# Layer 2's raw weights on GpSimd's DMA queue, their conversion's arithmetic behind the next step's gating

## The chip, the cores and the metric

One Trainium2 chip, one core of it. The metric is the device time of one launch in microseconds. The kernel before was run three times.

## The reference

Three parts follow one another on 3072 tokens of width 512, in float32; the inputs are given as 64-bit floats.

```python
for t in range(S):                       # B 4, H 8, S 768, D 64
    state = gamma * state + outer(k[t], v[t])
    y[t] = scale * q[t] @ state          # linear attention with decay per head
x = y as [3072, 512]
h = x @ w_in;  g = h * sigmoid(1.702 * h);  x = g @ w_out         # layer 1: 512 -> 2048 -> 512
h = x @ w_in2; P = a0 + a1 h + a2 h^2 + a3 h^3
Q = 1 + |b0| |h| + |b1| h^2;  out = (P / (Q + 1e-6)) @ w_out2     # layer 2: 512 -> 2048 -> 512
```

## The kernel before

Matrix products are made from a high and a low float32r part of each operand: three matmuls per product (high x low, low x high, high x high). So weights and activations must be split. A raw 64-bit weight is first turned into one float32 word by bit operations on ScalarE and VectorE.

Layer 1 runs in 96 steps: six blocks of 512 tokens, in each 16 chunks of 128 of the 2048 hidden columns. `step(i)` (L1538) works on two chunks at once: it issues the up-projection `g1(j)` of chunk j = i + 2 (12 matmuls of 128x512, L1122), its gating `act1_a(j)` (sigmoid on ScalarE, L1229; product z on VectorE, L1230), later the split of z into gh and gl by `act1_b(j)` (ScalarE L1238, VectorE L1239), and the down-projection `g2(i)` of chunk i (12 matmuls, L1143 to L1145). The up-projection's result stands in one of two PSUM banks (pool `ps_h`, tag "h", which attention's output `py` shares), so a bank is free for the next but one `g1` when z has been read out of it.

Between these stand the items of `todo[i]`: from block 1 on, attention's later chunks. `att_unit(c)` (L929) makes 64x64 matmuls (L954) for chunk c and chunk c + 1, then has SP fetch the turned q and k of c + 2 (`att_fetch`, L831) and load the raw q and k of c + 3 and the raw v of c + 2 (`load_raw`, L735). `att_turn(c)` (L812) scales and transposes q and k on VectorE (L816, L818) and has SP store them to DRAM (L823). The positions are counted in half-steps of a block (`UNIT_AT`, `TURN_IN`, L722 and L723): units at 1, 9, 17 and 25 with a turn 7 later; in the first such block, units at 9, 15, 21 and 25 and turns 5, 5, 3 and 7 later.

The conversion of layer 2's weights also runs beside layer 1: eight groups g, each of two chunks of w_in and two of w_out (units 4g to 4g + 3, 512 KB of raw words each). `conv2(g, x)` (L662) is the work of position x of a group, from x = -1 to 9; it is called at the end of step i with x = i - conv0[g] (L1573 to L1580), and conv0 is nine steps apart for the first groups and eight for the last. A raw unit is loaded by `raw2` (L622) at x = -1, 0, 3 and 5; `word2` (L634) makes the float32 word of it (ScalarE L561, then four operations on VectorE: L567, L569, L572, L583) at x = 0, 2, 5 and 7; `parts` and `whole` split it (ScalarE L619, VectorE L620), at x = 3 after four sums (L682); `put` (L649) stores the split weight to DRAM on GpSimd's queue at x = 2, 4, 6, 8 and 9, once per unit and once for the sums. Raw units, sums and other scratch share four slots (pool `ws`, tag "s"); a slot is free when the store that reads it has landed. `evac` takes two of them at the end of each block.

Each engine and each DMA queue works through its instructions in order. From step 14 to step 77 the orders of TensorE, VectorE, ScalarE and SP are the order in which the code issues them (`manual_schedule`, L1585); GpSimd's order isn't among them, but a DMA under `behind` (L613) stays after everything issued before it on its own engine. From step 78 on a planner orders all engines; there the sums and splits of layer 2's input are made (`x_piece`). Then layer 2 runs, from weights that it loads back from DRAM.

Of the kernel before, what the change touches and what calls it, by code (L numbers as in the profile page):

```python
# [18 lines left out]
P = 128  # L19
# [4 lines left out]
KD = DM // P  # L24
# [447 lines left out]
def tile_kernel(ctx: ExitStack, tc: tile.TileContext, q, k, v, w1i, w1o, w2i, w2o, pa, pb, cst, out):  # L472
    nc = tc.nc
# [47 lines left out]
    def unit(layer, u):  # L521
        return (ORD if layer == 1 else ORD2)[u]

    def stage_tag(u):

        if u < 16:
            at_slot = 31 - u
        elif u < 24:
            at_slot = 47 - u
        elif u < 28:  # L530
            at_slot = 55 - u
        elif u == 30:
            at_slot = 31
        else:
            return None
        return f"w{at_slot}"
# [49 lines left out]
    def w_high(layer, u, whole=True):  # L586
        nm, fc = unit(layer, u)
        if whole and layer == 1 and u in LATER:
            return
        m = STG[u]  # L590
        shape = [P, KD, P] if nm == "i" else [P, DM]
        if nm == "i":
            m = m.rearrange("p (c f) -> p c f", c=KD)
        pair = wp.tile([P, 2, *shape[1:]], F32R, tag=f"w{u}", name=f"w{nm}{layer}_{fc}")
        STG[u] = m
        W[layer, nm, fc] = (pair[:, 0], pair[:, 1])
        high = nc.scalar.copy(out=pair[:, 0], in_=m)
        if not whole:
            tc.keep_in_program_order(high)

    def w_low(layer, u, whole=True):
        if whole and layer == 1 and u in LATER:
            return
        hi, lo = W[layer, *unit(layer, u)]
        low = nc.vector.tensor_tensor(out=lo, in0=STG.pop(u), in1=hi.bitcast(F32), op=ALU.subtract)  # L605
        if not whole:
            tc.keep_in_program_order(low)

    NG = KF // 2
# [3 lines left out]
    def behind(dma):  # L613

        tc.keep_in_program_order(dma)
# [6 lines left out]
    def raw2(u):  # L622

        nm, f = unit(2, u)
        src = {"i": w2i, "o": w2o}[nm].bitcast(I32)
        s = ws.tile([P, DM, 2], I32, tag="s", name=f"s2_{u}")
        if nm == "i":
            src = src[:, f * 2 * P : (f + 1) * 2 * P].rearrange("(c p) f -> p c f", p=P)
            behind(nc.sync.dma_start(out=s.rearrange("p (c f) t -> p c (f t)", c=KD), in_=src))
        else:  # L630
            behind(nc.sync.dma_start(out=s.rearrange("p f t -> p (f t)"), in_=src[f * P : (f + 1) * P, :]))
        STG[u] = RW[u] = s

    def word2(u):  # L634
        w_first(u)
        w_bits(u)
        w_sign(u, False)
# [4 lines left out]
    def parts(key, src, home):  # L642

        n = src.shape[1] // (2 * P)
        t = home.bitcast(F32R).rearrange("p a b -> p (a b)").rearrange("p (x h c) -> p x h c", x=n, h=2)
        split((t[:, :, 0], t[:, :, 1]), src.rearrange("p (x c) -> p x c", c=2 * P))
        OUT2[key] = t

    def put(key):  # L649
        t = OUT2.pop(key)  # L650
        g, x = key
        if x == "o":
            nc.gpsimd.dma_start(out=WO[g], in_=t.bitcast(F32))
        else:
            nc.gpsimd.dma_start(out=WC[g][x].rearrange("x p h k f -> p x (h k f)"), in_=t.rearrange("p x h c -> p x (h c)").bitcast(F32))

    def whole(f, src, home):
        t = home.bitcast(F32R).rearrange("p a b -> p (a b)").rearrange("p (h c) -> p h c", h=2)
        split((t[:, 0], t[:, 1]), src)
        OUT2[f, "o"] = t  # L660

    def conv2(g, x):  # L662

        u = 4 * g
        if x == -1:
            raw2(u)
        elif x == 0:
            raw2(u + 1)
            word2(u)
        elif x == 1:  # L670
            parts((g, 0), STG[u], RW.pop(u))
        elif x == 2:
            put((g, 0))
            word2(u + 1)
        elif x == 3:
            raw2(u + 2)
            a, b = STG.pop(u), STG.pop(u + 1)
            a11, a12, a21, a22 = a[:, : 2 * P], a[:, 2 * P :], b[:, : 2 * P], b[:, 2 * P :]
            t = SUM[g] = ws.tile([P, 4, 2 * P], F32, tag="s", name=f"sum{g}")
            A22S[g] = a22  # L680
            for y, p, q, op in ((0, a21, a22, ALU.add), (1, t[:, 0], a11, ALU.subtract), (2, a11, a21, ALU.subtract), (3, a12, t[:, 1], ALU.subtract)):
                nc.vector.tensor_tensor(out=t[:, y], in0=p, in1=q, op=op)  # L682
            parts((g, 1), t[:, 0:2].rearrange("p x c -> p (x c)"), RW.pop(u + 1))
        elif x == 4:
            put((g, 1))
        elif x == 5:
            raw2(u + 3)
            word2(u + 2)
            t = SUM.pop(g)
            parts((g, 2), t[:, 2:4].rearrange("p x c -> p (x c)"), RW.pop(u + 2))  # L690
            parts((g, 3), A22S.pop(g), t[:, 0:2])
        elif x == 6:
            put((g, 2))
            put((g, 3))
        elif x == 7:
            word2(u + 3)
            e = ws.tile([P, DM, 2], I32, tag="s", name=f"wo{2 * g}s")
            whole(2 * g, STG.pop(u + 2), e)
        elif x == 8:
            put((2 * g, "o"))  # L700
            whole(2 * g + 1, STG.pop(u + 3), RW.pop(u + 3))
        elif x == 9:
            put((2 * g + 1, "o"))
# [409 lines left out]
    def g1(j):  # L1113
        layer, bi, fc, t0, n = steps[j]
        hp = ps_h.tile([P, n], F32, tag="h", name=f"hp{j}")
        wh, wl = W[layer, "i", fc]
        xh, xl = X[layer, bi]
        terms = [(kk, w, x) for kk in range(KD) for w, x in ((wl, xh), (wh, xl), (wh, xh))]
        if j == 0:
            terms.sort(key=lambda t: ((t[2] is xl) + (t[1] is wl or t[2] is xl), t[0]))  # L1120
        for x, (kk, w, t) in enumerate(terms):
            nc.tensor.matmul(hp, w[:, kk, :], t[kk // 2][:, kk % 2, :], start=(x == 0), stop=(x == len(terms) - 1))  # L1122
        HP[j] = hp
# [100 lines left out]
    def act1_a(j):  # L1224
        n = steps[j][4]
        hp = HP.pop(j)
        z = ch.tile([P, n], F32, tag="z", name=f"z{j}")
        CH[j] = z
        nc.scalar.activation(out=z, in_=hp, func=ACTF.Sigmoid, scale=1.702)  # L1229
        nc.vector.tensor_tensor(out=z, in0=hp, in1=z, op=ALU.mult)  # L1230
# [54 lines left out]
    for u in range(NU):  # L1285
        t = stage_tag(u)
# [10 lines left out]
    with tc.manual_schedule(engines={E.SP}):  # L1297
# [207 lines left out]
        conv0 = [KF + 2 + 9 * g - (0, 0, 0, 0, 1, 2, 3, 4)[g] for g in range(NG)]  # L1505
# [13 lines left out]
        def x_piece(i):  # L1519
            left = 2  # L1520
            while xq and left and (xq[0][0] or i > XS0 + 8):
# [10 lines left out]
                else:  # L1532
                    left -= 1
                    for f in xr[s, kk][n]:
                        if f:
                            f()

        def step(i):  # L1538
            nonlocal nxt, j
            while nxt < NS and nxt - lead[steps[nxt][0]] <= i:  # L1540
                j = nxt
                nxt += 1
                g1(j)
                act1_a(j)
            if 0 <= i - KF + 2 < WHOLE:
                w_high(1, LATER[i - KF + 2], False)
                w_low(1, LATER[i - KF + 2], False)
            if i == KF:
                tc.keep_in_program_order(nc.scalar.activation(out=ab[:, 6:7], in_=ab[:, 5:6], func=ACTF.Abs))
            late = [f() for f in todo[i][0]]  # L1550
            if j >= FIRST_STEPS + 2 and j in CH:
                act1_b(j)
            for f in late:
                if f:
                    f()
            g2(i)
            layer, bi, fc, t0, n = steps[i]
            if fc == KF - 1 and bi < 5:
                evac(bi)
            late = [f() for f in todo[i][1]]  # L1560

            if i >= XS0:
                x_piece(i)
            if i >= NS - 4:
                load_wo(2 * (i - NS + 4))
                load_wo(2 * (i - NS + 4) + 1)
            if i == XS0 + 4:
                for kk in range(2):
                    t = xp.tile([P, 2, 512], F32, tag=f"xh{kk}_0", name=f"xb{kk}")
                    XB.append(t)  # L1570
                    for c in range(2):
                        nc.sync.dma_start(out=t[:, c], in_=x2[4][2 * c + kk])
            for g in range(NG):  # L1573
                x = i - conv0[g]
                if x == 9:
                    conv2(g, x)
            for g in range(NG):
                x = i - conv0[g]
                if -1 <= x < 9:
                    conv2(g, x)  # L1580
            for f in late:
                if f:
                    f()
# [4 lines left out]
        for i in range(XS0, NS):  # L1588
            step(i)
# [32 lines left out]
```

## Time and profile before

| | |
|---|---|
| time, median of 3 | 1193.75 us (1192.49 to 1194.94) |
| the profiled execution | 1192.8 us, span 1191.0 us |
| TensorE busy | 1119.5 us, 94% of the span |
| VectorE busy | 868.8 us, 73% |
| ScalarE busy | 655.2 us, 55% |
| GpSimd busy | 31.1 us, 3% |
| DMA, SP's queue (hardware) | 169.27 MB, 49.4% of 16 engines |
| DMA, GpSimd's queue (software) | 23.07 MB, 5.3% of 16 engines |

The profile is of one execution. Its times count from the span's start. "L561" is line 561 of the code, PE is TensorE, PEld its weight loads, DVE VectorE, ACT ScalarE, POOL GpSimd, SPq the queue of SP. "a <- b" reads "a waited for b". The granted clock is given as a share of full speed: 1.00 is 2.4 GHz. Issuing a DMA isn't counted as busy time on SP.

### The profile page before, as it was taken

To read this page: it belongs to the slowest core of one execution; us is meant where nothing else is said; L and a number is where in the kernel's file an instruction comes from. 1 tells how busy PE (TensorE), PEld (TensorE's weight loads), DVE (VectorE), ACT (ScalarE), POOL (GpSimd) and SP (SyncE) were. 2 spreads that over 40 slices of the span, in tenths; PEclk is the share of its full clock that TensorE was granted. 3 is DMA by queue.
4 is the path that set the end of the run, shared out by engine and by line. 5 is a ranking of instruction groups with operands and counts; after the bars stand their busy time and mean duration, and the time that the engine had idled before them with its cause. 6 is when DMAs were issued, how large, how long until landed. Compare 5 with 4: busy or idle time off the path is not lost.

```text
span 1191.0 us, 18828 instructions
## 1 busy us (share of the span) xinstructions
PE 1119.5 (94%) x7217; PEld 911.8 (77%) x7217; DVE 868.8 (73%) x1192; ACT 655.2 (55%) x987; POOL 31.1 (3%) x52
## 2 busy tenths in 40 slices
PE   8999999698996879797999999999999999999998
PEld 6688878577775757586888888888888888888887
DVE  6999646375564445455577679999889899789895
ACT  5998322132232322222354569978778786787782
POOL 0000000000000000000000000000000000000000
PEclk9999999889998989899999999999999999999999
DMA  9944557565564554565278798583345561354100
GB/s 238 326 129 115 113 127 164 151 159 153 139 157 133 141 147 120 156 168 160 95 261 297 230 325 286 195 297 153 91 129 153 184 247 46 122 157 122 43 36 36
DMA packets 230394, 193.54 MB, mean 163 GB/s; under 512 B 153888, under 2 KB 178976, under 8 KB 230304
## 3 DMA queue, kind: packets, MB, share of 16 engines
q1 hardware_dynamic: 223904, 169.27, 49.4%
q0 software_dynamic: 6400, 23.07, 5.3%
q8 instruction: 57, 0.93, 0.3%
q14 instruction: 33, 0.27, 0.1%
HBM read 134.48 MB, written 57.67 MB: 161 GB/s over the span
## 4 chain that ended last, share of the span: by engine, by line
PE 66%; SPq 11%; DMA 9%; DVE 5%; issue 3%; ACT 2%; DVEq 0%; ACTq 0%
PE o L256 22%; PE hp L1122 13%; PE a L157 11%; SPq L735 7%; PE c L157 5%; DMA s<-in_moe_w_out_dram 4%; PE o L1143 3%; PE o L1144 3%; PE o L1145 3%; PE b L157 3%; DMA s<-in_moe_w_in_dram 2%; DMA xs<-x 2%; SPq L831 2%; SPq L823 1%; PE pY L954 1%
## 5 line engine op out<-in xcount | busy, mean ns | idle before, releaser
L1122 PE MATMUL hp<-xh,wi 128*128 128x512 f32 x768 | 266.7, 410 | 44.5 <-DVE z L1230 42.8
L1122 PEld LDWEIGHTS hp<-xh,wi 128*128 128x128 f32 x768 | 150.8, 196 | 81.8 <-DVE z L1230 45.9
L1122 PE MATMUL hp<-xl,wi 128*128 128x512 f32 x384 | 154.8, 404 | 0.0
L157 PE MATMUL a<-x,wi 128*128 128x512 f32 x576 | 145.3, 390 | 0.0
L1143 PE MATMUL o<-gh,wo 128*128 128x512 f32 x368 | 144.5, 393 | 0.0
L1144 PE MATMUL o<-gl,wo 128*128 128x512 f32 x368 | 143.6, 390 | 0.0
L1145 PE MATMUL o<-gh,wo 128*128 128x512 f32 x368 | 143.4, 390 | 0.0
L567 DVE TENSOR_SCALAR u<-u 128x512 f32<-128x512 f32 x64 | 27.0, 422 | 139.7 <-ACT u L561 139.7
L561 ACT ACTIVATE u<-s 128x512 f32<-128x512 f32 x64 | 43.1, 675 | 151.7 <-DMA s<-in_moe_w_in_dram 86.7
L157 PEld LDWEIGHTS a<-x,wi 128*128 128x128 f32 x576 | 108.0, 188 | 22.9 <-ACT b L180 0.4
L1238 ACT CAST gh<-z 128x512 fp32r<-128x512 f32 x80 | 49.6, 620 | 99.6 <-DVE z L1230 99.6
L1229 ACT ACTIVATE z<-hp 128x512 f32<-128x512 f32 x80 | 47.6, 595 | 86.3 <-PE hp L1122 80.1
L1230 DVE TENSOR_TENSOR z<-hp,z 128x512 f32<-128x512 f32 x80 | 54.9, 686 | 44.8 <-ACT z L1229 36.7
L1122 PEld LDWEIGHTS hp<-xl,wi 128*128 128x128 f32 x384 | 75.9, 198 | 15.2 <-issue 0.3
L320 DVE SCALAR_TENSOR_TENSOR z<-z,ab,w 128x1024 f32<-128x1024 f32 x48 | 61.6, 1283 | 28.4 <-ACT w L318 28.4
L1143 PEld LDWEIGHTS o<-gh,wo 128*128 128x128 f32 x368 | 69.7, 189 | 15.1 <-DVE wo L605 0.4
L1239 DVE TENSOR_TENSOR gl<-z,gh 128x512 fp32r<-128x512 f32 x80 | 54.7, 684 | 36.1 <-ACT gh L1238 35.0
L1144 PEld LDWEIGHTS o<-gl,wo 128*128 128x128 f32 x368 | 69.4, 189 | 14.6 <-DVE gl L1239 0.2
L1145 PEld LDWEIGHTS o<-gh,wo 128*128 128x128 f32 x368 | 69.2, 188 | 14.5
L157 PE MATMUL c<-x,wi 128*128 128x512 f32 x288 | 73.1, 389 | 0.0
L334 ACT ACTIVATE gh<-h 128x1024 fp32r<-128x1024 f32 x48 | 50.9, 1060 | 34.1 <-PE o L256 33.5
L338 DVE SCALAR_TENSOR_TENSOR gl<-h,gh 128x1024 fp32r<-128x1024 f32 x48 | 58.8, 1224 | 5.4 <-ACT gh L334 5.4
(246 smaller groups left out, 2203.5 us busy)
## 6 DMA issues: line engine op xcount, KB each, us to landing
wi<-wc SPq DMA_DIRECT2D x168, 256.0 KB, 2.9
s<-in_moe_w_in_dram SPq DMA_DIRECT2D x32, 512.0 KB, 5.6
s<-in_moe_w_out_dram SPq DMA_DIRECT2D x32, 512.0 KB, 5.2
x<-xc SPq DMA_DIRECT2D x28, 512.0 KB, 8.5
wc<-s POOLq DMA_DIRECT2D x24, 512.0 KB, 3.9
xc<-xo SPq DMA_DIRECT2D x36, 256.0 KB, 2.7
x<-os SPq DMA_DIRECT2D x20, 256.0 KB, 2.5
xs<-x SPq DMA_DIRECT2D x20, 256.0 KB, 4.3
```

Of the source, the lines that this page charges most:

```text
L157: nc.tensor.matmul(bank, wt[:, a, k], XT[s, x, k][:, b], start=begin and y == 0, stop=y == 5, skip_group_check=True)
L256: nc.tensor.matmul(ACC[d], a[:, x, r], w[:, b], start=g == 0 and x == 0 and y == 0, stop=g == NG - 1 and x == 1 and y == 2)
L320: dve("q", [("ab", m)], lambda: stt(out=v["z"], in0=v["z"], scalar=ab[:, 6:7], in1=v["w"], op0=ALU.mult, op1=ALU.add))
L334: nc.scalar.activation(out=GT[m][0], in_=h, func=ACTF.Copy, scale=-1.0)
L338: nc.vector.scalar_tensor_tensor(out=gl, in0=h, scalar=-1.0, in1=gh.bitcast(F32), op0=ALU.mult, op1=ALU.subtract)
L735: nc.sync.dma_start(out=t[HALF[n], NP * x : NP * x + NP, :], in_=heads[x])
L1122: nc.tensor.matmul(hp, w[:, kk, :], t[kk // 2][:, kk % 2, :], start=(x == 0), stop=(x == len(terms) - 1))
L1143: nc.tensor.matmul(o, wl[:, r], gh, start=a, stop=False)
L1144: nc.tensor.matmul(o, wh[:, r], gl, start=False, stop=False)
L1145: nc.tensor.matmul(o, wh[:, r], gh, start=False, stop=z)
L1230: nc.vector.tensor_tensor(out=z, in0=hp, in1=z, op=ALU.mult)
L1239: nc.vector.tensor_tensor(out=gl, in0=z, in1=gh.bitcast(F32), op=ALU.subtract)
```

## The change

The raw units of layer 2 are loaded from GpSimd's queue, not SP's. `conv2` is cut in two: `conv2_load` issues the load of a position where `conv2` was called, at the end of step i; the arithmetic and the stores of that position are called by `convert(i - 1)` in the next step, behind its `g1` and `act1_a` and ahead of its attention items, its `act1_b` and its `g2`.

```diff
         if nm == "i":
...
-            behind(nc.sync.dma_start(out=s.rearrange("p (c f) t -> p c (f t)", c=KD), in_=src))
+            behind(nc.gpsimd.dma_start(out=s.rearrange("p (c f) t -> p c (f t)", c=KD), in_=src))
         else:
-            behind(nc.sync.dma_start(out=s.rearrange("p f t -> p (f t)"), in_=src[f * P : (f + 1) * P, :]))
+            behind(nc.gpsimd.dma_start(out=s.rearrange("p f t -> p (f t)"), in_=src[f * P : (f + 1) * P, :]))
...
+    def conv2_load(g, x):
+
+        n = {-1: 0, 0: 1, 3: 2, 5: 3}.get(x)
+        if n is not None:
+            raw2(4 * g + n)
+
     def conv2(g, x):
         u = 4 * g
-        if x == -1:
-            raw2(u)
-        elif x == 0:
-            raw2(u + 1)
+        if x == 0:
             word2(u)
...
         elif x == 3:
-            raw2(u + 2)
...
         elif x == 5:
-            raw2(u + 3)
             word2(u + 2)
...
+        def convert(i):
+            for g in sorted(range(NG), key=lambda g: i - conv0[g] != 9):
+                if 0 <= i - conv0[g] <= 9:
+                    conv2(g, i - conv0[g])
+
         def step(i):
...
                 g1(j)
                 act1_a(j)
+            convert(i - 1)
...
             for g in range(NG):
-                x = i - conv0[g]
-                if x == 9:
-                    conv2(g, x)
-            for g in range(NG):
-                x = i - conv0[g]
-                if -1 <= x < 9:
-                    conv2(g, x)
+                conv2_load(g, i - conv0[g])
```

## Rows read from the trace of the kernel before

**Rows 1.** Times by stage: from:to, length, busy of each engine, clock, DMA share, GB/s.
```profile
160.00:630.00 470.00, 406.70 (x3426) 334.07 (x3425) 261.43 (x477) 133.96 (x251) 29.10 (x45) 0.93 0.57 153
600.00:630.00 30.00, 30.00 (x134) 24.86 (x133) 23.67 (x44) 15.67 (x28) 2.59 (x5) 1.00 0.66 245
630.00:692.00 62.00, 61.73 (x272) 50.55 (x271) 41.62 (x67) 29.61 (x51) 1.83 (x3) 1.00 0.83 284
```
**Rows 2.** Waits of TensorE, 160 to 630 us: total, times, longest.
```profile
PE hp L1122 <- DVE z L1230: 42.5, 9, 9.6
PE pY L954 <- DVE z L1230: 17.2, 6, 4.1
PE pK L954 <- DMA rawv<-in_v_dram: 3.1, 1, 3.1
```
**Rows 3.** Waits of ScalarE for layer 2's raw weights, same stretch.
```profile
ACT u L561 <- DMA s<-in_moe_w_in_dram: 86.7, 7, 15.5
...
ACT u L561 <- DMA s<-in_moe_w_out_dram: 56.5, 8, 10.4
```
**Rows 4.** The chain of waits, 205 to 240 us: start, length, what.
```profile
215.40 5.46 PE hp L1122 x12
...
223.63 2.72 PE hp L1122 x12
...
232.64 4.73 DMA s<-in_moe_w_in_dram
237.39 0.67 ACT u L561
...
238.88 0.70 DVE u L572
```
**Rows 5.** SP's queue in order of time, one attention round: start, length.
```profile
216.71 1.78 SPq L823 DMA_DIRECT2D tq<-turnq  x4
...
220.52 1.66 SPq L831 DMA_DIRECT2D qT<-tq  x2
...
223.96 2.84 SPq L735 DMA_DIRECT2D rawq<-in_q_dram  x4
...
229.57 2.96 SPq L735 DMA_DIRECT2D rawv<-in_v_dram  x4
232.64 1.09 SPq L629 DMA_DIRECT2D s<-in_moe_w_in_dram  x2
```
**Rows 6.** Attention's matmuls (L954) by stage: busy and count, TensorE first.
```profile
160.00:200.00 40.00, 4.40 (x256) 4.12 (x256) 1.00 0.60 148
160.00:630.00 470.00, 41.93 (x1904) 39.11 (x1904) 0.93 0.57 153
```
**Rows 7.** GpSimd in order of time: start, length, idle before.
```profile
196.94 0.72 POOL L655 DMA_DIRECT2D wc<-s  x1 [10.85 <-DVE s L620]
197.66 0.57 POOL L655 DMA_DIRECT2D wc<-sum  x1
```
**Rows 8.** DMA issues, KB each, median us to landing; last, of L629's loads.
```profile
wc<-s POOLq DMA_DIRECT2D x24, 512.0 KB, 3.9
...
rawk<-in_k_dram SPq DMA_DIRECT2D x64, 64.0 KB, 2.7
...
tq<-turnq SPq DMA_DIRECT2D x64, 64.0 KB, 1.8
...
DMA to landing us min/median/max: 3.8/4.9/6.3
```
**Rows 9.** Groups by line, whole span: count, busy us, mean ns.
```profile
L1239 DVE TENSOR_TENSOR gl<-z,gh 128x512 fp32r<-128x512 f32 x80 | 54.7, 684 | 36.1 <-ACT gh L1238 35.0 <-PE o L1145 0.7
...
L1238 ACT CAST gh<-z 128x512 fp32r<-128x512 f32 x80 | 49.6, 620 | 99.6 <-DVE z L1230 99.6
...
L572 DVE SCALAR_TENSOR_TENSOR u<-u,s 128x512 int32<-128x512 int32 x64 | 44.3, 693 | 3.9 <-ACT s L555 0.2
...
L567 DVE TENSOR_SCALAR u<-u 128x512 f32<-128x512 f32 x64 | 27.0, 422 | 139.7 <-ACT u L561 139.7
...
L818 DVE STREAM_TRANSPOSE turnk<-rawk 128x512 f32<-128x512 f32 x16 | 11.4, 711 | 0.6
```

## The prediction, made before the change was run

> **What bounds the kernel now.** I read the times by stage first, then the waits of the engine that is full elsewhere, then one stall in the chain of waits, then the queue that it names. TensorE is full at the end of layer 1, every microsecond of 600 to 630 and 61.73 of the 62.00 after. From 160 to 630 us it works 406.70 of 470.00 us at a mean granted clock of 0.93 [rows 1]. So 63.3 us are idle there, and part of the busy time ran at the lower of its two levels, 1.2 GHz: one group of 12 matmuls took 5.46 us right after a stall, and 2.72 us when none had gone before [rows 4]. How much that is: in 160 to 200 us, at clock 1.00, 256 small attention matmuls took 4.40 us, 0.0172 each; a large one takes 2.72/12 = 0.2267. The 3426 matmuls of the stage hold 1904 small ones [rows 6], so 1522 large: 1522 x 0.2267 + 1904 x 0.0172 = 345.0 + 32.7 = 377.7 us. Busy was 406.7, so the low clock cost 29.0 us. Stall and clock together: 92.3 us that this stage would not need.
>
> Why it stalls: 42.5 + 17.2 us of 63.3 wait for VectorE's gating product z (L1230), 15 times [rows 2]; in the same stretch ScalarE waits 15 times, 143.2 us, for a raw weight of layer 2 to land [rows 3]. The chain shows how one becomes the other: raw weight on its way at 232.64, landed 237.39, ScalarE's first conversion op then, VectorE's conversion at 238.88 [rows 4]; the next step's sigmoid and z stand behind them on their queues, and a PSUM bank is free only after z. And the weight is late because its issue on SP stands behind a whole attention round: turn stores from 216.71, fetches from 220.52, 12 raw q/k/v loads from 223.96, and only at 232.64 the weight [rows 5]: 15.9 us of queue ahead of a transfer that lands in 4.9 [rows 8].
>
> **The change, part by part.**
> 1. *32 loads leave SP.* SP no longer puts them behind attention rounds. What is left in front of them is Pool's queue, which holds only the conversion's own stores, 48 of them at 0.72 us (two-part weights) or 0.57 (one part) [rows 7]. On Pool a load of w_in is four pieces of 128 rows; with 0.57 for 128 and 0.72 for 256 I estimate 0.57 + 3 x 0.15 = 1.0 us of issue, w_out 0.57. Not shown by the trace: a load from this queue. Its landing I bound by 3.8 (the fastest raw load from SP) and 6.3 (the slowest), and take 4.9, the middle of rows of the same bytes [rows 8].
> 2. *How early they now come.* Each load's slot (four of them) comes free when a store has landed: store issue 0.7, landing 3.9 [rows 8], load 1.0, landing 4.9: 10.5 us after the data of that store are ready. A step is 24 matmuls, 5.44 us, so 1.9 steps. By the schedule the stores' data are made at x = 1, 3 and 5, and the loads that they make room for are used at x = 5, at 7 and at 0 of the next group: four steps on, three for the last where groups are eight steps apart. 3 x 5.44 = 16.3 against 10.5 plus at most one step in which the data are made, 15.9: covered everywhere, by 0.4 us at the tightest (three or four places), by 5 us elsewhere. I price it at nothing; without cover it costs its excess four times.
> 3. *Arithmetic behind the next step's gating.* Nothing added or dropped; ScalarE and VectorE get each step's conversion after z(j) and ahead of the split of z(j), instead of ahead of z(j+1). A late weight would now hold up the split, not z. The split's deadline is the down-projection of j, four groups of 12 after the up-projection of j: 10.9 us. Longest load in front of it: sigmoid and product, like gh and gl, 1.3; word2 0.67 on ScalarE and 2 x 0.42 + 2 x 0.69 = 2.2 on VectorE; two part splits, 1.1 more on VectorE; a turn of four ops of at most 0.71, 2.8; then gh 0.62 and gl 0.68 [rows 4, 9]: 9.4 us. Covered by 1.5 us; without cover some 2 us in the heaviest step of each of 8 groups, 16 us. Below nothing it can't go, since the loads already take away what z waited for; I take 0 to 3.
> 4. *Pool's stores* are issued as soon as their data are there, as now, but stand behind loads that may wait for a slot. Nobody but the next loads and the far-off layer 2 waits for them.
>
> *What is late next.* Attention's ring on SP: turn 2.8, its stores 3.8, landing 1.8, fetch 3.4, raw q and k 2/3 of 8.7 = 5.8, landing 2.7 [rows 5, 8, 9]: 20.3 us per unit, to the next turn. TensorE needs 4 x 5.44 + 119 x 0.0172 = 23.8 us per unit: covered by 3.5. Only in the first block, where the turn at position 20 holds up the loads of the unit at 21 and the unit at 25 needs its raw v, it isn't: 5 x 2.72 + 2.0 = 15.6 us against turn to landed raw v, 2.8 + 3.8 + 1.8 + 3.4 + 8.7 + 2.7 = 23.2. That leaves a stall of 7.6 us, which the wait of TensorE for raw v, 3.1 us today [rows 2], grows into; with one group at the low clock after it (5.46 - 2.72 = 2.7) some 10 us. To that I add 5 us for landings that lengthen because the same bytes move in less time (DMA share 0.57 x 470/378 = 0.71; it was 0.83 in the next stage, where nothing stalled [rows 1]); the 5 is an estimate from the spread of 3.8 to 6.3.
>
> Sum against the profiled execution: 1192.8 us (span 1191.0 and 1.8 around it) - 92.3 + 10 + 5 = 1115.5. That execution lies 0.95 under the median of three, 1193.75: forecast 1116.5, say 1117 us.
>
> *A rule that speaks against.* Row first: 15.9 us of issues stand before the weight on SP, and the transfer itself is 4.7 [rows 4, 5]. The Trainium skill, "DMA: Bandwidth & Descriptors", section "Issuing engines are not separate DMA queues", says that DMAs of all issuing engines share the same 16 engines and that issuing from several saves only the sequencer's issue time, usually small. By it the gain would be the issues alone, rival E below. The trace agrees that bytes aren't the limit here (share 0.57 [rows 1]), but issue time is not small: it is what is long. So I keep the sum.
>
> **Rivals.**
> - *A, SP's attention ring becomes the pace.* For: the DMAs now overlap, and the ring has 3.5 us of room. Against: SP loses 32 issues. If its issues and landings, 17.5 of the 20.3, get 40% longer, the ring is 27.3, 3.5 over, for 16 units 56 us, and 10 for the first block: 1192.8 - 92.3 + 66 = 1166.
> - *B, slower: Pool's queue turns into a serial ring.* Place: the four slots in 160 to 630. If each load waits for the landing of the store just issued, and the next store for that load's arithmetic, a group costs 4 x (0.7 + 3.9 + 1.0 + 4.9) + 4 x 3 of arithmetic = 54 us, against 9 x 5.44 + 2.25 x 2.0 = 53.5 of TensorE: just hidden. It decides from landings a third longer: the ring is then 66, and 8 x 12 eats the 92. At landings half as long again it is 71.6, 18 x 8 = 145 us of stalls: 1192.8 - 92.3 + 145 = 1245. Against: loads are issued two steps ahead, so the ring isn't serial. The Trainium skill, "SBUF — State Buffer", section "SBUF: two separate sides", says that descriptors of a Pool DMA can't be written while VectorE holds the shared port in its two-port mode; the stores so far took 0.72 and 0.57 beside a VectorE that is busy 261 of 470 us [rows 1, 7], so no row shows it.
> - *C, no effect: the loads are as late as now*, held behind stores that wait for arithmetic: 1194. Against: point 2.
> - *D, the split of z comes late* (point 3): 1117 + 16 and the clock after each stall, 8 x 2.7: 1155.
> - *E, only the issues are saved*: the weights then wait for bytes among attention's instead of behind its issues; 32 x 0.5 us [rows 5]: 1192.8 - 16 = 1177. Against: a DMA share of 0.57 in this stage.
>
> **How the numbers follow.** Forecast 0.72, A 0.10, E 0.03, D 0.05, C 0.03, B 0.07. The forecast's own range is 1101 (all 92 us gone) to 1135 (residue twice as large). With D and the nearer half of A it reaches 1150; left out are half of A, E, B, C and a little at the edges, under 2 in 10: 1099 to 1150. What a measurement of this kernel can tell from no change is 0.2%, 2.4 us. Faster: forecast, A, E, D: 0.90; same: C and a little, 0.03; slower: B, 0.07.
>
> **What would show it.** Right: in the stage after 160 us TensorE idles under 20 us, its clock is 0.97 or more, and the stage is 70 to 90 us shorter; ScalarE's waits for raw weights fall from 143 to under 15 us; SP's rounds end with raw v; what stall is left stands in the first attention block and names raw v or a turn. Layer 2, full before [rows 1], is unchanged. Wrong: waits of u for s remain, now from Pool's loads, with Pool idle on a store's landing (B, C); ScalarE or VectorE waiting on attention's raws in every unit (A); TensorE waiting for gl at the down-projection (D).

## The result, and the profile after

The changed kernel takes 1117.08 us (median of 4, 1116.53 to 1119.67) against 1194.35 for the kernel before, timed beside it: a ratio of 0.9357, interval 0.9336 to 0.9379. The forecast was 1117. The span of the profiled execution fell from 1191.0 to 1114.8 us, by 76.2.

Times by stage of the changed kernel (length, busy of TensorE, its weight loads, VectorE, ScalarE, GpSimd, then clock, DMA share, GB/s). The work that filled 160 to 630 us [rows 1] now fills 160 to 553:

```profile
160.00:553.00 393.00, 386.90 (x3435) 320.02 (x3434) 261.97 (x477) 134.30 (x251) 49.28 (x76) 0.99 0.68 181
...
200.00:240.00 40.00, 35.06 (x358) 28.76 (x357) 22.58 (x41) 10.51 (x22) 5.03 (x8) 0.91 0.77 190
240.00:280.00 40.00, 38.84 (x392) 31.89 (x391) 27.16 (x49) 13.18 (x25) 5.21 (x8) 1.00 0.69 190
280.00:553.00 273.00, 273.00 (x2275) 226.21 (x2274) 185.62 (x340) 98.01 (x183) 36.32 (x56) 1.00 0.69 186
```

About as many TensorE instructions as in [rows 1] (3435 and 3426, with the window's edges) take 77 us less. From 280 to 553 us TensorE isn't idle for a moment, and what is left of the stall stands in 200 to 280 us. VectorE and ScalarE do the same work as before, 262 and 134 us. Behind this stage nothing changed: 561.8 us to the end of the span, 561.0 before.

The waits of TensorE in that stage, which answer to [rows 2]:

```profile
PE pK L955 <- DMA rawv<-in_v_dram: 4.9, 3, 2.0
PE o L1144 <- DVE os L1156: 1.2, 1, 1.2
```

The 59.7 us for z are gone; raw v, 3.1 us before, is the main wait. All waits of ScalarE and VectorE for layer 2's raw weights, 143 to 600 us (143.2 us on ScalarE in [rows 3]):

```profile
DVE s L569 <- DMA s<-in_moe_w_out_dram: 5.4, 2, 2.8
ACT u L561 <- DMA s<-in_moe_w_out_dram: 2.1, 1, 2.1
DVE s L569 <- DMA s<-in_moe_w_in_dram: 0.7, 1, 0.7
```

GpSimd in order of time (start, length, idle before and what ended it): stores and loads in turn, and a load that waits 2.87 us for a store to land, as the prediction's point 2 has it:

```profile
183.36 0.71 POOL L655 DMA_DIRECT2D wc<-s  x1 [13.53 <-DVE s L620]
184.07 0.58 POOL L631 DMA_DIRECT2D s<-in_moe_w_out_dram  x1
199.84 0.72 POOL L655 DMA_DIRECT2D wc<-s  x1 [15.20 <-DVE sum L620]
200.56 0.58 POOL L655 DMA_DIRECT2D wc<-sum  x1
204.01 0.75 POOL L629 DMA_DIRECT2D s<-in_moe_w_in_dram  x1 [2.87 <-DMA wc<-s]
```

SP's queue in the first attention block: this round ends with raw v, and the next one follows at once, so SP has no room here:

```profile
214.67 1.00 SPq L832 DMA_DIRECT2D qT<-tq  x2
...
217.35 2.77 SPq L736 DMA_DIRECT2D rawq<-in_q_dram  x4
...
222.89 2.57 SPq L736 DMA_DIRECT2D rawv<-in_v_dram  x4
225.56 2.52 SPq L824 DMA_DIRECT2D tq<-turnq  x4
```

The chain of waits there (start, length, what): raw v lands, attention's matmul starts, and the next group of 12 runs in part at the lower clock, 4.49 us in place of 2.72. One attention unit later it happens again, with 3.57 us:

```profile
205.01 4.41 DMA rawv<-in_v_dram
...
209.46 0.27 PE pK L955
...
210.51 4.49 PE hp L1123 x12
...
224.19 3.40 DMA rawv<-in_v_dram
...
229.59 3.57 PE hp L1123 x12
```

DMA issues by group, KB each, median us to landing, beside [rows 8]. The raw weights land in 5.2 and 6.1 us from GpSimd's queue; some of attention's own transfers, which now run beside them, take longer: a turn's stores of q 3.8 where it was 1.8, raw k 3.4 where it was 2.7. Others don't: raw q 3.2 where it was 3.1, the fetches of q 3.4 as before.

```profile
s<-in_moe_w_in_dram POOLq DMA_DIRECT2D x16, 512.0 KB, 5.2
s<-in_moe_w_out_dram POOLq DMA_DIRECT2D x16, 512.0 KB, 6.1
...
rawk<-in_k_dram SPq DMA_DIRECT2D x64, 64.0 KB, 3.4
...
tq<-turnq SPq DMA_DIRECT2D x64, 64.0 KB, 3.8
```

### The profile page after: what moved, and what is told of

It is laid out like the page before. It is cut to its first block, busy times and chain, and to the rows that moved or that the text cites. A ratio compares the mean times of both kernels' runs of the same rounds, so it can differ in the third digit from the quotient of the medians.

```text
span 1114.8 us, 18800 instructions
## 1 busy us (share of the span) xinstructions
PE 1098.4 (99%) x7216; PEld 895.8 (80%) x7217; DVE 868.8 (78%) x1192; ACT 654.7 (59%) x987; POOL 52.3 (5%) x84
## 3 DMA queue, kind: packets, MB, share of 16 engines
q1 hardware_dynamic: 213152, 152.49, 48.1%
q0 software_dynamic: 11008, 39.85, 11.0%
## 4 chain that ended last, share of the span: by engine, by line
PE 84%; DMA 5%; SPq 3%; DVE 2%; issue 1%; ACT 1%; POOL 0%; DVEq 0%; ACTq 0%
PE o L256 23%; PE hp L1123 19%; PE a L157 12%; PE c L157 6%; PE o L1144 6%; PE o L1145 6%; PE o L1146 6%; PE b L157 3%; SPq L736 2%; PE pY L955 2%; DMA xc<-xo 2%; PE o L1142 1%; DMA rawv<-in_v_dram 1%; DMA xs<-x 1%; DMA tq<-turnq 1%
## 5 line engine op out<-in xcount | busy, mean ns | idle before, releaser
L1123 PE MATMUL hp<-xh,wi 128*128 128x512 f32 x768 | 256.8, 396 | 1.8 <-DVE wi L605 0.8
L1123 PEld LDWEIGHTS hp<-xh,wi 128*128 128x128 f32 x768 | 145.2, 189 | 35.6 <-DVE z L1231 2.0
L1123 PE MATMUL hp<-xl,wi 128*128 128x512 f32 x384 | 150.0, 392 | 0.0
L1144 PE MATMUL o<-gh,wo 128*128 128x512 f32 x368 | 144.0, 391 | 1.2 <-DVE os L1156 1.2
L1145 PE MATMUL o<-gl,wo 128*128 128x512 f32 x368 | 143.4, 390 | 1.1 <-DVE gl L1240 1.1
L1123 PEld LDWEIGHTS hp<-xl,wi 128*128 128x128 f32 x384 | 72.7, 189 | 14.2
L1144 PEld LDWEIGHTS o<-gh,wo 128*128 128x128 f32 x368 | 69.1, 188 | 16.5 <-DVE os L1156 1.6
L1145 PEld LDWEIGHTS o<-gl,wo 128*128 128x128 f32 x368 | 69.1, 188 | 15.6 <-DVE gl L1240 1.5
L157 PEld LDWEIGHTS c<-x,wi 128*128 128x128 f32 x288 | 54.1, 188 | 11.2
L321 ACT ACTIVATE w<-z,ab 128x1024 f32<-128x1024 f32 x48 | 55.1, 1152 | 12.2 <-DVE z L320 12.2
```

Source lines behind the costliest of these rows:

```text
L157: nc.tensor.matmul(bank, wt[:, a, k], XT[s, x, k][:, b], start=begin and y == 0, stop=y == 5, skip_group_check=True)
L321: act("rs", [("q", m)], lambda: A(out=v["w"], in_=v["z"], func=ACTF.Abs_reciprocal_sqrt, bias=ab[:, 7:8]))
L1144: nc.tensor.matmul(o, wl[:, r], gh, start=a, stop=False)
L1145: nc.tensor.matmul(o, wh[:, r], gl, start=False, stop=False)
```

## The experiments

The kernels ran in three sets: the first four below, the next four, the last two. The kernel before was timed again beside each set and took 1189.0 to 1189.3 us, where it had taken 1194.35 beside the result. So ratios to it are given, and times are compared within one set.

**Each edit alone.** Two theories: Q, a weight is late because it is issued behind an attention round on SP; G, what pays is that z no longer stands behind the conversion. First the loads alone: the loads on GpSimd's queue, the arithmetic back at the step's end.

```diff
-            convert(i - 1)
...
                 conv2_load(g, i - conv0[g])
+            convert(i)
```

> The loads on GpSimd's queue, the arithmetic at a step's end as before. Theory Q (a raw weight is late because it is issued behind an attention round on SP; nothing else makes z late): the whole gain is here, 1110 to 1120 us, ScalarE waits under 15 us for raw weights. Rival G (what pays is that z no longer stands behind the conversion): 1150 to 1175 us, with z still behind conversions that wait. If both edits are needed, something between, near 1140.

Measured: 1112.38 us, ratio 0.9346 (0.9317 to 0.9375). TensorE's waits, 100 to 640 us:

```profile
PE pK L955 <- DMA rawv<-in_v_dram: 3.1, 2, 2.5
PE hp L1123 <- DVE z L1231: 1.4, 4, 0.5
```

z is waited for 1.4 us, though it stands behind a conversion as before. Q holds, G falls: the loads alone give the whole gain.

Then the arithmetic alone: behind the next gating, the loads on SP where they were.

```diff
-            behind(nc.gpsimd.dma_start(out=s.rearrange(...), in_=src))
+            behind(nc.sync.dma_start(out=s.rearrange(...), in_=src))
```

> The arithmetic behind the next step's gating, the loads on SP at the place where they were. Theory Q: the weights land as late as before, ScalarE still waits some 100 us for them; the wait now holds up the split of z, which has one group of matmuls more of room, so part of the stalls goes: 1150 to 1175 us, and TensorE's waits name gl at the down-projection in place of z at the up-projection. Rival G: 1115 to 1130 us.

Measured: 1160.89 us, ratio 0.9758 (0.9726 to 0.979). The late weights are still there, in ScalarE's waits from 143 to 620 us:

```profile
ACT u L561 <- DMA s<-in_moe_w_in_dram: 74.6, 7, 15.5
ACT u L561 <- DMA s<-in_moe_w_out_dram: 26.0, 8, 4.7
```

TensorE now waits mainly in other places, at the down-projection (L1144, L1145), for ScalarE and for gh and gl. The expectation had named gl alone. The longest of its waits:

```profile
PE o L1144 <- ACT z L1230: 20.5, 2, 11.5
PE pK L955 <- DMA rawv<-in_v_dram: 6.1, 3, 4.5
PE o L1144 <- ACT gh L1239: 3.6, 1, 3.6
PE o L1145 <- DVE gl L1240: 3.2, 2, 1.7
```

So the move softens a late weight: it is worth 28 us of the kernel before. That this comes from the one group of matmuls more until the split is needed fits the changed places, but isn't shown by itself.

**Which queue, or which place in it.** The loads stay on SP and the arithmetic at the step's end; each load is issued one position earlier, at the head of the step, ahead of its attention items.

```diff
                 act1_a(j)
+            for g in range(NG):
+                conv2_load(g, i + 1 - conv0[g])
...
-                conv2_load(g, i - conv0[g])
+            convert(i)
```

> The loads stay on SP, the arithmetic stays at a step's end; each load is issued one position earlier and at the head of the step, ahead of the step's attention items. Theory Q (it is the order on the queue, not which queue): 1112 to 1130 us; a load that waits for its slot now holds up attention's DMAs, which may cost some us. Rival S (it takes a queue of its own): 1160 us or more, since the weights still share SP with 12 loads per attention unit.

Measured: 1118.18 us, ratio 0.9397 (0.9373 to 0.9422). SP has all its DMAs back, and nearly all of the gain stays. ScalarE waits 5.4 us for weights. It takes 5.8 us more than the loads on GpSimd's queue in the same set. A likely cause is that a load which waits for its slot now holds up SP, and TensorE waits 6.2 us for raw v where it waited 3.1; how much of the 5.8 us this makes isn't shown. That wait of SP, over the span:

```profile
SPq L629 <- DMA wc<-s: 34.1, 5, 14.0
```

This agrees with the Trainium skill, "DMA: Bandwidth & Descriptors", section "Issuing engines are not separate DMA queues", in that DMAs issued by different engines run on the same 16 DMA engines, so that a queue of its own adds little: 5.8 us beside a good place on SP. Against what the prediction weighed it for (rival E), the place in a queue is worth 70 us here.

**The rest of the stall.** The changed kernel with a unit's raw v ahead of its raw q and k.

```diff
+            if FLAT < c and c + 2 <= LASTC:
+                load_raw(c + 2, "v")
             if c + 3 <= LASTC:
                 load_raw(c + 3, "q")
                 load_raw(c + 3, "k")
-            if FLAT < c and c + 2 <= LASTC:
-                load_raw(c + 2, "v")
```

> The changed kernel with a unit's raw v loaded ahead of its raw q and k (same bytes). The changed kernel's last stalls are TensorE's 4.9 us for raw v, with a low clock after them (0.91 in 200 to 240 us). Theory (the raw v stands last in SP's round): the wait for raw v goes, 5 to 10 us less than the changed kernel, 1107 to 1113 us. Rival (the round as a whole is late, so the turn that waits for raw k is late instead): 1115 to 1120 us, with VectorE waiting for raw k.

Measured: 1114.85 us, ratio 0.9367 (0.9338 to 0.9397): not to be told from the changed kernel. TensorE's wait for raw v is nearly gone, and others stand in its place:

```profile
PE hp L1123 <- ACT z L1230: 2.9, 1, 2.9
PE o L1145 <- DVE gl L1240: 2.2, 1, 2.2
PE o L1144 <- DVE os L1156: 1.7, 1, 1.7
PE pS L955 <- DMA kT<-tk: 1.6, 1, 1.6
PE pK L955 <- DMA rawv<-in_v_dram: 0.3, 1, 0.3
```

The theory, 1107 to 1113 us, fell. The rival fits, since the round as a whole stays late, but its sign doesn't tell the two apart: VectorE waits 3.3 us for raw k ahead of a turn (L817), and 3.7 in the changed kernel. What is new is 7.0 us for raw q at the same place, which the changed kernel doesn't have.

**Twice the load.** The changed kernel with every raw weight loaded twice into its slot.

```diff
-            behind(nc.gpsimd.dma_start(...))
+            for _ in range(2):
+                behind(nc.gpsimd.dma_start(...))
```

> The changed kernel with every raw weight loaded twice into its slot, the second load after the first has landed: a weight is there some 6 us later (one issue and one landing of 5.2 or 6.1 us more), 16.8 MB more are moved. By point 2 of the prediction (a cover of 0.4 us at three or four places, 5 us elsewhere): three or four stalls of up to 6 us and little ones elsewhere, 10 to 30 us more than the changed kernel. Rival (the loads are further ahead than that): within 3 us of it. Rival B (Pool's queue is a serial ring): 32 x 6 us less the 54 - 53 that was hidden, over 100 us more.

Beside it ran the changed kernel once more:

> The changed kernel as it is, beside the kernels of the same call. 0.936 of the time before, as measured.

Measured: 1138.3 us, ratio 0.9562 (0.954 to 0.9584), against 1117.65 and 0.9391 (0.937 to 0.9412): 21 us more. The changed kernel took as long as before, 1117.65 and 1117.08; its ratio lies above the 0.936 that was expected, because the kernel before was faster beside it. The 21 us are of the size that point 2 gives, but only a part of them comes by its mechanism. Waits of the run, 143 to 600 us:

```profile
PE pK L957 <- DMA rawv<-in_v_dram: 12.3, 4, 6.3
PE hp L1125 <- DVE z L1233: 3.7, 3, 2.0
PE o L1146 <- ACT gh L1241: 3.3, 1, 3.3
...
ACT u L561 <- DMA s<-in_moe_w_out_dram: 5.4, 2, 4.1
ACT u L561 <- DMA s<-in_moe_w_in_dram: 4.0, 1, 4.0
```

Two things show. TensorE waits 12.3 us for raw v, at a DMA share of 0.80 where it was 0.68; in two traced executions of the changed kernel it waited 4.9 and 5.8. And ScalarE waits 9.4 us for the weights, VectorE 7.3, and TensorE 7.9 us for z, gh and gl (1.7 and 0.5 in the changed kernel). TensorE's waits for these all lie after 540 us, where the last group is converted. The chain of waits there (start, length, what) leads from the doubled load of a weight to z and the up-projection:

```profile
561.65 5.96 DMA s<-in_moe_w_out_dram
...
567.63 0.57 ACT u L561
568.20 0.61 ACT z L1232
...
568.83 0.70 DVE z L1233
...
569.58 3.03 PE hp L1125 x12
```

So weights some 6 us later are covered in most places and reach TensorE in the last group, which is one of the tightest places of point 2; and attention's transfers are late beside the doubled bytes. How the 21 us divide, this run can't say, since it changed both. The 100 us of rival B's serial ring aren't there.

**Toward a faster version.** The loads alone again, as the base.

> The loads on GpSimd's queue, the arithmetic at a step's end: the base of the kernel with even units. Theory Q: the moved arithmetic is worth nothing or costs 1 to 4 us, since gh and gl then stand behind a conversion, so 0 to 4 us less than the changed kernel. Rival G: 0 to 4 us more.

Measured: 1111.72 us (1111.15 to 1112.78), ratio 0.9344 (0.9323 to 0.9364), 5.9 us under the changed kernel in the same set (1116.23 to 1118.46): the two groups of times don't overlap, nor do the intervals of the ratios. So the moved arithmetic costs some 5 us. The earlier pair agrees in its times (1117.08 and 1112.38), while its ratios, 0.9357 and 0.9346, have intervals that overlap. Two kinds of waits of the changed kernel are gone or small with the loads alone, each in two traced executions. ScalarE and VectorE wait 8.2 and 8.2 us for raw weights (143 to 600 us), against 0 and 0.8. And the copies of a finished block out of PSUM (`evac`) wait for a slot, VectorE's 2.4 us (none with the loads alone) and ScalarE's 3.3 (0.6 and 0.8). These last in the changed kernel, 100 to 600 us:

```profile
DVE os L1156 <- DMA wc<-s: 2.4, 1, 2.4
...
ACT os L1154 <- DMA wc<-s: 3.3, 1, 3.3
```

TensorE feels 1.2 us of it directly, and waits 4.9 and 5.8 us for raw v in the changed kernel against 3.1 and 3.8 with the loads alone. All its waits from 100 to 640 us come to 7.8 and 8.1 us, against 4.5 and 5.3. The spans of the profiled executions differ by 2.3 and 3.5 us, about as much as these waits; the medians differ by more, and the rest of the 5 us isn't accounted for.

Now the first block's units, evenly spaced:

```diff
-UNIT_AT = ([1, 9, 17, 25], [9, 15, 21, 25])
+UNIT_AT = ([1, 9, 17, 25], [7, 13, 19, 25])
-TURN_IN = ([7, 7, 7, 7], [5, 5, 3, 7])
+TURN_IN = ([7, 7, 7, 7], [5, 5, 5, 7])
-            here += [(0, enter), (8, lambda: att_turn(FLAT + 2))]
+            here += [(0, enter), (6, lambda: att_turn(FLAT + 2))]
```

> The loads on GpSimd's queue, the arithmetic at a step's end, and the first attention block's units spaced evenly: at 7, 13, 19 and 25, turns at 6, 12, 18, 24 and 32, in place of 9, 15, 21 and 25 and turns at 8, 14, 20, 24 and 32. Theory (what is left of the stall is the first block's ring, 23 us against 15.6 where turns stand four half-steps apart): with six, 18.3 and for raw v 21, the stall of some 3 us and the low clock after it go, 3 to 8 us less than with the loads alone, 1104 to 1110 us where that gives 1112. Rival (the ring is late in every distance under eight half-steps, so the stall is only spread): within 2 us of it.

Measured: 1110.37 us (1105.3 to 1112.23), ratio 0.9322 (0.9295 to 0.9348). The median is 1.4 us under the loads alone, which is the rival's "within 2 us" and not the theory's 3 to 8. Its traced execution still has a wait of 3.1 us for a raw v in the first block, so a third kernel loads a unit's raws ahead of the fetch, and the even units ran again beside it.

```diff
-            if c + 2 <= LASTC:
-                att_fetch(c + 2)
...
                 load_raw(c + 3, "k")
+            if c + 2 <= LASTC:
+                att_fetch(c + 2)
```

> The kernel with even units and the loads alone moved, and in each attention unit the raw v, q and k loaded ahead of the fetch of turned q and k. In the run with even units TensorE still waited 3.1 us for a raw v that SP issued 12 us after VectorE's turn, behind that turn's stores, their landing and the fetch. Theory (the raw loads needn't stand behind the fetch): that wait goes, with the low clock after it 4 to 7 us less than with even units alone. Rival (the fetch, now 8 us later, is waited for instead): within 2 us of it, TensorE waiting for qT or kT.

> The kernel with even units again, beside the one with the raw loads first: 0.930 to 0.935 of the time before.

Measured: raws first 1110.61 us, ratio 0.9347 (0.9325 to 0.9369), with TensorE waiting 3.8 us for a fetched k in the place of raw v. So the theory fell, and the rival had the wait right, though the time is 4 us above the even units and not within 2. Even units again: 1106.58 us (1105.73 to 1112.02), ratio 0.9324 (0.93 to 0.9348). The profiled execution of the latter took 1106.06 us, and its middle stage is full:

```profile
160.00:553.00 393.00, 392.89 (x3479) 325.44 (x3478) 269.79 (x487) 139.53 (x257) 50.34 (x78) 1.00 0.71 191
```

The even units' executions lie between 1105.3 and 1112.2 us. Of the two that were traced, the one of 1106.06 has no wait for raw v and the one of 1112.23 has; whether that parts the others too isn't shown. By their medians they are the fastest version; their gain over the loads alone, 0.9322 and 0.9324 against 0.9344 with intervals that overlap, is likely and not shown.

## Why the prediction was right, point by point

- *What bounds the kernel*: right in kind and size. The stage held 92.3 us that it didn't need, 77 of them went. The stage is now 393 us against 377.7 of needed TensorE time: a residue of 15.3, where 10 + 5 was forecast. 6.1 of it is idle (393.0 - 386.9) and 3.6 the low clock (0.09 of 40 us); the window's edges hold some 9 more large matmuls than I counted, 2.0; the small matmuls took 2.7 more than at full clock (35.4 and 32.7), part of it the same low clock. That the forecast was met to a tenth of a microsecond is in part luck: raw v and the clock behind it cost some 8.5 (4.9 and 3.6) where 10 was forecast, the 5 for longer landings is seen nowhere by itself, and the 5 of point 3 were not in the sum. With the loads alone, without point 3, the time was 1112, 5 us under the forecast. The range's upper end is not worked out right either: a residue of 30 in place of 15 gives 1131.5 and not 1135, which changes nothing here.
- *Point 1*: issue on GpSimd 0.76 us for w_in where I estimated 1.0, and 0.57 as estimated for w_out; landing 5.2 and 6.1 in the median, within 3.8 to 6.3, though single loads of w_out took up to 7.8.
- *Point 2*: right in what it priced, nothing, and not quite in "covered everywhere". In four places ScalarE or VectorE waits for a weight, 8.2 us in all and 2.8 at most, and none of it reaches TensorE in the stage. With the loads alone it is 0 and 0.8 us, so these waits come with the moved arithmetic, which point 2 didn't count. The 0.4 us at the tightest places wasn't tested by itself; with doubled loads the last group is where it broke.
- *Point 3*: the term that was wrong. I took 0 to 3 us and looked only at the deadline of the split, which held: no wait for gl in the stage. The move costs some 5 us. What I left out is that `convert` takes a group's stores along, so slots come free later, for `evac` at a block's end and for the next loads. At the end of the first attention block the split of the sums starts 1.2 us ahead of VectorE's first copy of `evac`; with the loads alone it was 3.8. The traces show both waits; how they make up the cost is open.
- *What is late next*: right in nature and block, raw v in the first attention block. It is 4.9 us where I worked out 7.6, and at two units in a row, 2.0 and 3.0, where I had one; two groups behind them were slow, 4.49 and 3.57 us. The 5 us for longer landings are not shown: a turn's stores of q went from 1.8 to 3.8 us and raw k from 2.7 to 3.4, but raw q and the fetches of q stayed, and with the loads alone, which move the same bytes, raw k took 2.6 and 2.5.
- *Rivals*: E is refuted by the result and by the loads issued early on SP; C by 8.2 us of waits where it needed 143; B's loss didn't come even with each weight loaded twice; A is seen only in the first block, where one round on SP follows another without a gap; D in a small form, not by way of gl. On the rule behind B, the Trainium skill, "SBUF — State Buffer", section "SBUF: two separate sides": the 16 loads of w_in took 753 to 900 ns to issue, median 762, beside a VectorE that was busy 262 of 393 us, so no lockout shows in the issue. Loads of w_out did land later from this queue than from SP at the same DMA share (below); whether the rule has a part in that, no run tells.

## What to carry to other kernels

When an engine waits for a DMA that itself lands in 5 us, look at what stands ahead of its issue: here 15.9 us of other transfers' issues on an in-order queue, which first made two engines wait, then the third, and then cost its clock as well. Moving the issue earlier in the same queue is worth nearly as much as a queue of its own. A second edit that softens the same wait should be timed by itself: here it was worth 28 us alone and cost some 5 us once the first was in.

## What the runs showed of the hardware that was not expected

The same 16.8 MB of raw weights make fewer packets from GpSimd's queue: SP's packets fell by 10752 (223904 to 213152), GpSimd's rose by 4608 (6400 to 11008). And loads of the same size landed about as fast from either queue in one shape and not in the other. The run with the loads early on SP compares them at the same DMA share, 0.68: w_in took 5.5 us from SP and 5.2 from GpSimd's queue, w_out 4.4 from SP and 6.1 from GpSimd's (5.6 and 5.8 with the loads alone). Why w_out differs isn't shown.
